# One store of eight rows instead of two of four, in a decode kernel fed by one stream of loads

## The chip, the cores and the metric

The kernel runs on one core of one Trainium2 chip. Its time is the device time of one execution in microseconds; smaller is better. Five engines work side by side: TensorE (PE, with its weight loads listed apart as PEld), VectorE (DVE), ScalarE (ACT), GpSimd (POOL) and SyncE (SP). SP and ACT each have a queue on which they issue transfers, and all transfers run on the same 16 DMA engines. SBUF and PSUM are the core's memories of 128 partitions (rows).

## What is computed

One decode step of a transformer block for two sequences, in float32. `x` has shape (2, 1, 512). It is normalised, and three terms are added:

```python
xn = _layernorm(x, axis=-1)
return x + _A_ref(xn, K, V, wq, wo) + _B_ref(xn, w_gate, w_up, w_down)
```

The term A is attention with 32 heads of 128: `q = xn @ wq`, scores of q against the last 2048 of 8192 cached keys, softmax, the weighted sum of the cached values, and `@ wo`. The term B is `((xn @ w_gate) * (xn @ w_up)) @ w_down` with 1376 inner columns. For each of the 2 x 32 pairs of sequence and head some 1 MB of keys and 1 MB of values is read once. With the weights that is 159.5 MB to load, and 4 KB to store.

## The kernel before

**The stream.** The host lays caches and weights out in the order of use, in one array `stream`. `blocks()` (line 38) lists the pieces: keys of head h, values of head h - 3 (`LAG`), the slices of `wq` and `wo` that go with them, and at the end the pieces of `w_down` (`wd`). `pump()` (line 139) issues these loads on SP's queue into a ring of three step tiles, each of 55,296 bytes on each partition. `done()` (line 164) counts the users of a tile and calls `pump()` when a tile is free. The first load, `wq0`, has a tile of its own. The last load, `wd_rest`, brings the last 96 rows of `w_down`.

**The order on an engine.** `InOrder` (line 73) keeps each engine's instructions in the order in which they are written; all calls through it appear in the profile as line 85. POOL is not wrapped, so its lines (181, 198, 278, 294) appear by themselves. The main loop (line 400) takes one head's keys, multiplies them on DVE by q (`products`, in place), sums over the 128 columns (`sums`), takes maxima, and lets ACT make the exponentials into a ring of tiles `p`. The head's values follow three heads later on PE (`weigh`, `pv`). `transpose(h)` then picks the two sequences' rows with a small table of ones, `pick`, and ACT scales them into `oT`, of 128 rows and 2 columns, the weights of `project_o`.

**The sum.** `project_o` sums into two rows (one for each sequence) of the PSUM tile `acc`, 512 columns wide, for the heads before `HF` = 26. Then the sum is spread: `accumulate` (line 300) cuts the 512 columns into four groups g of 128 and writes group g to the rows 32 g and 32 g + 1, so that four narrow matmuls use four parts of the array. The sum so far is copied to `acc_sb` and put in through the identity. The last heads and all of `w_down` (`down`, with `hT` as weights) go this way. `keep_busy` issues matmuls whose result is not used.

**The two ends.** `x_t` (line 122) is one tile with three parts, brought by one load on ACT's queue: x with its 512 columns spread over partitions (`xT`, 8 columns), x in the rows 32 g + b where the result will stand (`x_nat`, 128 columns, zero elsewhere), and `pick` (8 columns). The mean and variance come from `xT`, then `xn` and its copies `xnb`, which PE uses for the first q. At the end DVE adds `x_nat` to the whole spread sum, 128 by 128 (line 474), and the result leaves in two stores, one for each sequence, of four rows of 512 bytes each: sequence 0 on SP's queue, sequence 1 on ACT's.

Of the kernel before, what the change touches and what calls it, by code (L numbers as in the profile page):

```python
# [8 lines left out]
F32 = mybir.dt.float32  # L9
AF = mybir.ActivationFunctionType  # L10
# [6 lines left out]
P = 128  # L17
B, D, H, DH, SK, F = 2, 512, 32, 128, 8192, 1376
W = min(4096, max(256, SK // 4))
J = W // P  # L20
NC = D // P
FB = 4 * P
NFB = -(-F // FB)
NFC = F // P
FR = F - NFC * P
FH = [(0, 2 * FB), (2 * FB, F)]
LAG = 3
HG = 4
GC = HG * DH
JG = J // 4  # L30
# [7 lines left out]
def blocks():  # L38
# [6 lines left out]
    def k(h):  # L45
        first = [("w", 1, CQ - NC * DH)] if h == 0 else []
        return [("k", h, CK)] + first + ([("wq", h, CP)] if h + HG < H else [])

    def v(h):
        return [("v", h, CK), ("wo", h, CO)]  # L50

    def gu(half):
        n = NC * (FH[half][1] - FH[half][0])
        return [("wg", half, n), ("wu", half, n)]

    units = []
    for h in range(LAG, H - 1):
        units += [k(h), v(h - LAG)]
    loads = [k(0), gu(0) + k(1), gu(1) + k(2), units[0] + units[1]]
    loads += [sum(units[i : i + 3], []) for i in range(2, len(units), 3)]  # L60
    loads += [k(H - 1) + v(H - 1 - LAG)]
    out = [(("q", 0), [("w", 0, NC * DH)])]
# [38 lines left out]
def kernel(  # L101
    ctx: ExitStack,
    tc: tile.TileContext,
    x: bass.AP,
    stream: bass.AP,
    wd_rest: bass.AP,
    out: bass.AP,
):
    nc = tc.nc
    pe, dve, act, sp = (InOrder(tc, e) for e in (nc.tensor, nc.vector, nc.scalar, nc.sync))  # L110
# [3 lines left out]
    const = ctx.enter_context(tc.tile_pool(name="const", bufs=1))  # L114
    steps = ctx.enter_context(tc.tile_pool(name="steps", bufs=BUFS))
    small = ctx.enter_context(tc.tile_pool(name="small", bufs=6))
# [2 lines left out]

    x_t = const.tile([P, B * NC + P + 4 * B], F32, name="x_t")
    act.dma_start(x_t, x)
    xT = x_t[:, 0 : B * NC].rearrange("p (b c) -> p b c", b=B)
    x_nat = x_t[:, B * NC : B * NC + P]
    pick = x_t[:, B * NC + P :].rearrange("p (r b) -> p r b", b=B)


    todo, at = [], 0
# [34 lines left out]
    def done(kind, i):  # L164
# [14 lines left out]
    ident = const.tile([P, P], F32, name="ident")  # L179
    nc.gpsimd.memset(ident, 1.0)  # L180
    nc.gpsimd.affine_select(
        out=ident, in_=ident, compare_op=ALU.is_equal, fill=0.0, base=0,
# [2 lines left out]

    acc_t = ps_c.tile([P, D], F32, name="acc")
    dve.memset(acc_t, 0.0)
    acc, acc_g = acc_t[:B, :], acc_t[:, :P]

    o_ps = [ps_c.tile([P, 4 * DH], F32, name=f"o_ps{i}") for i in range(2)]  # L190
    for t in o_ps:
# [2 lines left out]

    NP = LAG + 2
    p_ring = [const.tile([P, B, JG, 4 * B], F32, name=f"p{i}") for i in range(NP)]
    for t in p_ring:
        nc.gpsimd.memset(t, 0.0)


# [24 lines left out]
    q_ps, s_t, mm_t, p_t, sum_t, rec_t, o_sbs, oT = {}, {}, {}, {}, {}, {}, {}, {}  # L225
# [4 lines left out]
    def project_first(i):  # L230
        w = got["w", i][0].rearrange("p (c n) -> p c n", c=NC)
        if i == 0:
            q = q_first
        else:
            q_ps[0] = ps_q.tile([P, B, GC], F32, name="q")
            q = q_ps[0][:, :, DH:]
        for b in range(B):
            for c in range(NC):
                pe.matmul(
                    q[:, b, :], xnb[:, c * B + b, :], w[:, c, :],  # L240
                    start=(c == 0), stop=(c == NC - 1),
                )
        done("w", i)

    def project_q(h):

        g, c = h // HG + 1, h % HG
        if c == 0:
            q_ps[g] = ps_q.tile([P, B, GC], F32, name="q")
        for b in range(B):  # L250
            pe.matmul(
                q_ps[g][:, b, :], xnb[:, c * B + b, :], got["wq", h][0],
                start=(c == 0), stop=(c == NC - 1),
            )
        done("wq", h)

    def k_of(h):
        return got["k", h][0].rearrange("p (b j d) -> p b j d", b=B, j=J)

    def products(h):  # L260
        g, hh = divmod(h, HG)
        kt = k_of(h)
        qb = q_ps[g][:, :, hh * DH : (hh + 1) * DH] if h else q_first
        dve.tensor_tensor(
            kt, kt, qb.unsqueeze(2).to_broadcast([P, B, J, DH]), op=ALU.mult
        )
# [33 lines left out]
    def accumulate(lhsT, rhs, last=False):  # L300
        nonlocal n_acc
        for g in range(4):
            pe.matmul(
                acc_g[32 * g : 32 * g + B, :], lhsT, rhs[:, g * P : (g + 1) * P],
                start=(n_acc == 0), stop=last,
            )
        n_acc += 1

    def keep_busy(n):
        pe.matmul(spare[:, 0:n], mean_w, spare_in[:, 0:n], start=True, stop=True)  # L310
# [14 lines left out]
    def transpose(h):  # L325
        o_sb, rec = o_sbs.pop(h), rec_t.pop(h)
        d = tr[:, 8 + 4 * (h % 2) : 8 + 4 * (h % 2) + B]
        for r in range(4):
            pe.matmul(
                d, o_sb[:, r * DH : (r + 1) * DH], pick[:, r, :],  # L330
                start=(r == 0), stop=(r == 3),
            )
        oT[h] = small.tile([P, B], F32, name="oT")
        for b in range(B):
            act.activation(
                oT[h][:, b : b + 1], d[:, b : b + 1], AF.Copy, scale=rec[:, b : b + 1]
            )

    def project_o(h):
        wo = got["wo", h][0]  # L340
        if h < HF:
            pe.matmul(acc, oT.pop(h), wo, start=(h == 0), stop=(h == HF - 1))
        else:
            accumulate(oT.pop(h), wo)
        done("wo", h)
# [15 lines left out]
        project_o(h)  # L361


    hT = const.tile([P, 4, 4, B], F32, name="hT")

    def project_gu(half):
        lo, hi = FH[half]
# [12 lines left out]
    def gate():  # L380
        g_sb = small.tile([P, FB], F32, name="o_sb", bufs=2)
        act.copy(g_sb, gu_ps[0])
        h_sb = small.tile([P, FB], F32, name="o_sb", bufs=2)
        dve.tensor_tensor(h_sb, g_sb, gu_ps[1], op=ALU.mult)
        for i in range(4):
            t = tr[:, (i % 3 + 1) * P : (i % 3 + 2) * P]
            pe.transpose(t, h_sb[:, i * P : (i + 1) * P], ident)
            act.copy(
                hT[:, i, :, :], t.rearrange("p (n r) -> p n r", r=32)[:, :, 0:B]
            )  # L390

    def down(n):
# [7 lines left out]
    for _, fields in blocks()[1:]:  # L400
# [6 lines left out]
        for n, h in enumerate(ks):  # L407
            products(h)
            if h == 0:
                project_first(1)  # L410
            if h + HG < H:
                project_q(h)
# [14 lines left out]

    h = H - 2
    spare = ps_q.tile([P, B, GC], F32, name="q")[:, 0, :]
    acc_sb = const.tile([B, D], F32, name="acc_sb")  # L430
    dve.tensor_copy(acc_sb, acc)
    products(h)
    sums(h)
# [1 line left out]
    pv(HF + 1)  # L435
    keep_busy(GC)
    transpose(HF)
    accumulate(ident[:B, :B], acc_sb)
    keep_busy(256)
    project_o(HF)  # L440
    transpose(HF + 1)
# [30 lines left out]
    accumulate(hT[:FR, NFC % 4, NFC // 4, :], got["wd", NFC][0][:FR], last=True)  # L472
    o_out = const.tile([P, P], F32, name="o_out")
    dve.tensor_tensor(o_out, acc_g, x_nat, op=ALU.add)
    for b, eng in ((0, sp), (1, act)):
        eng.dma_start(out[b, 0, :].rearrange("(g n) -> g n", n=P), o_out[b::32, :])


def laid_out(x):

    import numpy as np

    a = x["A_x"].reshape(B, D)
    xs = np.zeros((P, B * NC + P + 4 * B), a.dtype)
    xs[:, : B * NC] = a.reshape(B, P, NC).transpose(1, 0, 2).reshape(P, B * NC)
    for b in range(B):
        xs[b::32, B * NC : B * NC + P] = a[b].reshape(D // P, P)
        for r in range(4):
            xs[4 * b + r :: 32, B * NC + P + r * B + b] = 1.0
    cache = {  # L490
        kind: x[name][:, :, SK - W :, :].reshape(B, H, P, J * DH).transpose(1, 2, 0, 3)
        for kind, name in (("k", "A_k_cache"), ("v", "A_v_cache"))
    }
    wq = x["A_wq"].reshape(P, NC, H // HG, GC).transpose(2, 0, 1, 3)
    wo = x["A_wo"].reshape(H, P, D)
    gu = {
        kind: x[name].reshape(P, NC, F)
        for kind, name in (("wg", "B_w_gate"), ("wu", "B_w_up"))
    }
    wd = x["B_w_down"]  # L500

    def field(kind, i):
        if kind in ("k", "v"):
            return cache[kind][i].reshape(P, CK)
        if kind in ("v0", "v1"):
            return cache["v"][i].reshape(P, B, -1)[:, int(kind[1])]
        if kind == "w":
            return (wq[0][:, :, DH:] if i else wq[0][:, :, :DH]).reshape(P, -1)
        if kind == "wq":
            return wq[i // HG + 1][:, i % HG, :]  # L510
        if kind == "wo":
            return wo[i]
        if kind == "wd":
            return wd[i * P : (i + 1) * P]
        return gu[kind][:, :, FH[i][0] : FH[i][1]].reshape(P, -1)

    parts = [
        np.concatenate([field(kind, i) for kind, i, _ in fields], axis=1).ravel()
        for _, fields in blocks()
    ]  # L520
    return {"x": xs, "stream": np.concatenate(parts), "wd_rest": wd[NFC * P :]}


_INS = ["A_x", "A_k_cache", "A_v_cache", "A_wq", "A_wo", "B_w_gate", "B_w_up", "B_w_down"]
# [28 lines left out]
```

## Time and profile before

| | |
|---|---|
| median of 3 runs | 380.98 us (380.95 to 381.12) |
| profiled execution | 380.88 us, span 378.8 us |
| PE busy | 264.5 us (70%) |
| DVE busy | 293.9 us (78%) |
| ACT busy | 64.0 us (17%) |
| POOL busy | 25.4 us (7%) |
| read from HBM | 159.52 MB, 421 GB/s over the span |

The page gives the busy time of each engine, then the span in 40 slices with one digit each (the busy share in tenths), then the DMA queues with their packets, bytes and share of 16 DMA engines' time: q1 is SP's queue, q10 ACT's. A group of instructions is written as line, engine, operation, output <- inputs, with shapes as partitions x elements; after the bar stand the busy time and the mean of one in nanoseconds, and then the idle time of the engine just ahead of them with what ended it. In an extract in order of time the columns are start and duration in microseconds, engine, line, operation, tiles, and in square brackets the idle time before it. The span is the profiled part of an execution; 2.1 us of the time lie around it.

### The profile page before, as it was taken

To read this page: it belongs to the slowest core of one execution; us is meant where nothing else is said; L and a number is where in the kernel's file an instruction comes from. 1 tells how busy PE (TensorE), PEld (TensorE's weight loads), DVE (VectorE), ACT (ScalarE), POOL (GpSimd) and SP (SyncE) were. 2 spreads that over 40 slices of the span, in tenths; PEclk is the share of its full clock that TensorE was granted. 3 is DMA by queue.
4 is the path that set the end of the run, shared out by engine and by line. 5 is a ranking of instruction groups with operands and counts; after the bars stand their busy time and mean duration, and the time that the engine had idled before them with its cause. 6 is when DMAs were issued, how large, how long until landed. Compare 5 with 4: busy or idle time off the path is not lost.

```text
span 378.8 us, 3075 instructions
## 1 busy us (share of the span) xinstructions
PE 264.5 (70%) x1188; PEld 92.7 (24%) x1188; DVE 293.9 (78%) x143; ACT 64.0 (17%) x264; POOL 25.4 (7%) x75
## 2 busy tenths in 40 slices
PE   3949882757838875684886668488477847719996
PEld 3512221212212221221222122122112311203342
DVE  3739892996799499589949949994994998699920
ACT  1020020102101110210121121021203112202221
POOL 0000000000000000000000000010000000000000
PEclk9978985868876696986679687768958879757999
DMA  8999999999999999999999999999999999999993
GB/s 321 458 419 435 438 445 444 403 444 461 389 450 450 403 455 420 428 455 403 439 457 391 455 450 393 461 421 426 455 415 428 455 423 433 400 445 408 426 415 146
DMA packets 4893, 159.71 MB, mean 422 GB/s; under 512 B 552, under 2 KB 688, under 8 KB 1296
## 3 DMA queue, kind: packets, MB, share of 16 engines
q1 hardware_dynamic: 4728, 159.45, 98.0%
q8 instruction: 9, 0.15, 0.2%
q10 hardware_dynamic: 152, 0.08, 0.1%
q14 instruction: 4, 0.03, 0.0%
HBM read 159.52 MB, written 0.00 MB: 421 GB/s over the span
## 4 chain that ended last, share of the span: by engine, by line
DMA 54%; DVE 31%; PE 11%; ACT 2%; issue 1%; SPq 0%; POOL 0%; DVEq 0%
DMA step<-in_stream_dram 54%; DVE s L85 15%; DVE step L85 15%; PE acc L85 3%; PE o_ps L85 3%; PE q L85 2%; PE tr L85 2%; ACT o_sb L85 1%; ACT oT L85 1%; DVE m L85 0%; SPq L85 0%; ACT p L85 0%; DVE rec L85 0%; POOL mm L278 0%; DVE acc_sb L85 0%
## 5 line engine op out<-in xcount | busy, mean ns | idle before, releaser
L85 DVE TENSOR_TENSOR step<-step,q 128x4096 f32<-128x4096 f32 x31 | 136.6, 4407 | 57.8 <-DMA step<-in_stream_dram 52.4
L85 DVE TENSOR_REDUCE s<-step 128x32 f32<-128x4096 f32 x32 | 141.4, 4420 | 1.1
L85 PE MATMUL q<-step,xnb 128*128 128x512 f32 (+1 forms) x128 | 91.9, 864 | 58.2 <-DMA step<-in_stream_dram 58.1
L85 PE MATMUL o_ps<-step,p 128*8 128x512 f32 x512 | 85.1, 725 | 8.2 <-DMA step<-in_stream_dram 8.0
L85 PEld LDWEIGHTS q<-step,xnb 128*128 128x128 f32 x128 | 32.1, 274 | 112.8 <-issue 55.7
L85 PE MATMUL tr<-x_t,o_sb 128*128 128x2 f32 x256 | 33.3, 252 | 22.9 <-ACT o_sb L85 22.8
L85 PE MATMUL acc<-step,oT 128*2 128x512 f32 (+1 forms) x100 | 38.2, 535 | 13.1 <-ACT oT L85 13.1
L85 PEld LDWEIGHTS tr<-x_t,o_sb 128*128 128x128 f32 x256 | 31.2, 191 | 51.3 <-ACT o_sb L85 50.6
L85 ACT COPY o_sb<-o_ps 128x512 f32<-128x512 f32 x33 | 19.2, 583 | 114.0 <-PE o_ps L85 114.0
L85 PEld LDWEIGHTS o_ps<-step,p 128*8 128x8 f32 x512 | 14.0, 97 | 73.6 <-issue 62.4
L85 ACT ACTIVATE nm<-mm 128x2 f32<-128x2 f32 x32 | 6.5, 203 | 147.2 <-POOL mm L278 147.2
L278 POOL PARTITION_ALL_REDUCE mm<-m x32 | 11.4, 357 | 285.4 <-DVE rec L85 184.4
L85 ACT ACTIVATE oT<-tr,rec 128x1 f32<-128x1 f32 x64 | 13.2, 257 | 37.6 <-PE tr L85 37.6
L85 ACT ACTIVATE p<-s,nm 128x16 f32<-128x16 f32 x64 | 19.2, 300 | 1.0
L294 POOL PARTITION_ALL_REDUCE sum<-rs x32 | 12.8, 400 | 41.6 <-ACT p L85 41.6
L85 ACT ACTIVATION_READ_ACCUMULATOR p<-s,nm 128x1 f32 x64 | 12.0, 187 | 0.0
L85 PE MATMUL o_ps<-step,xn 128*2 128x512 f32 (+1 forms) x48 | 11.9, 548 | 0.0
L85 PE MATMUL q<-xnb,mean_w 128*128 128x512 f32 (+1 forms) x24 | 11.9, 584 | 0.0
L85 DVE TENSOR_TENSOR o_out<-acc,x_t 128x128 f32<-128x128 f32 x1 | 0.3, 292 | 11.3 <-PE acc L85 11.3
L85 DVE TENSOR_TENSOR step<-step,tr 128x4096 f32<-128x4096 f32 x1 | 4.4, 4420 | 4.4 <-DMA step<-in_stream_dram 4.4
L85 PEld LDWEIGHTS acc<-step,oT 128*2 128x2 f32 x100 | 3.1, 82 | 17.9 <-ACT oT L85 16.8
L85 DVE TENSOR_REDUCE m<-s 128x2 f32<-128x32 f32 x32 | 5.9, 186 | 1.1
(36 smaller groups left out, 37.9 us busy)
## 6 DMA issues: line engine op xcount, KB each, us to landing
step<-in_stream_dram SPq DMA_DIRECT2D x16, 6912.0 KB, 31.7
step<-in_stream_dram SPq DMA_DIRECT2D x2, 6400.0 KB, 30.6
step<-in_stream_dram SPq DMA_DIRECT2D x1, 6656.0 KB, 29.2
step<-in_stream_dram SPq DMA_DIRECT2D x1, 4608.0 KB, 25.3
step<-in_stream_dram SPq DMA_DIRECT2D x2, 2304.0 KB, 13.5
step<-in_stream_dram SPq DMA_DIRECT2D x1, 4352.0 KB, 24.9
step<-in_stream_dram SPq DMA_DIRECT2D x1, 3712.0 KB, 33.8
step<-in_stream_dram SPq DMA_DIRECT2D x1, 3072.0 KB
```

What stands on the lines that cost most here:

```text
L85: made = call(*args, **kwargs)
L278: nc.gpsimd.partition_all_reduce(mm, m, P, bass_isa.ReduceOp.max)
L294: nc.gpsimd.partition_all_reduce(sum_t[h], rs, P, bass_isa.ReduceOp.add)
```

## The change

The result leaves in one store of eight rows on SP. For that, sequence 1 is summed in row 32 g + 16 of `acc` rather than 32 g + 1, so that the rows wanted are every 16th. The weights of these sums get 17 columns rather than 2, where columns 1 to 15 are zero: `oT` becomes a ring of three tiles cleared once by POOL, `hT` grows from 2 to 17 columns for each chunk and is cleared once by DVE, `acc_sb` has 17 rows and the identity is 17 by 17. The one load of `x_t` is cut into four on ACT's queue: `x_t` (128 rows of 32 bytes), `pick` (the same size), and four rows of 512 bytes for each sequence into `x_nat`, which DVE clears first.

```diff
+RB = 16
+M = RB * (B - 1) + 1
...
-    x_t = const.tile([P, B * NC + P + 4 * B], F32, name="x_t")
+    x_t = const.tile([P, B * NC], F32, name="x_t")
     act.dma_start(x_t, x)
...
+    pick_t = const.tile([P, 4 * B], F32, name="pick")
+    act.dma_start(pick_t, picks)
+    pick = pick_t.rearrange("p (r b) -> p r b", b=B)
+    x_nat = const.tile([P, P], F32, name="x_nat")
+    dve.memset(x_nat, 0.0)
+    for b in range(B):
+        act.dma_start(x_nat[RB * b :: 32, :], x_rows[b])
...
-    acc, acc_g = acc_t[:B, :], acc_t[:, :P]
+    acc, acc_g = acc_t[:M, :], acc_t[:, :P]
...
+    oT_ring = [const.tile([P, M], F32, name=f"oT{i}") for i in range(3)]
+    for t in oT_ring:
         nc.gpsimd.memset(t, 0.0)
...
-                acc_g[32 * g : 32 * g + B, :], lhsT, rhs[:, g * P : (g + 1) * P],
+                acc_g[32 * g : 32 * g + M, :], lhsT, rhs[:, g * P : (g + 1) * P],
...
-        oT[h] = small.tile([P, B], F32, name="oT")
+        oT[h] = oT_ring[h % 3]
         for b in range(B):
             act.activation(
-                oT[h][:, b : b + 1], d[:, b : b + 1], AF.Copy, scale=rec[:, b : b + 1]
+                oT[h][:, RB * b : RB * b + 1], d[:, b : b + 1], AF.Copy, scale=rec[:, b : b + 1]
             )
...
-    hT = const.tile([P, 4, 4, B], F32, name="hT")
+    hT = const.tile([P, 4, 4, M], F32, name="hT")
+    dve.memset(hT, 0.0)
...
-                hT[:, i, :, :], t.rearrange("p (n r) -> p n r", r=32)[:, :, 0:B]
+                hT[:, i, :, ::RB], t.rearrange("p (n r) -> p n r", r=32)[:, :, 0:B]
...
-    acc_sb = const.tile([B, D], F32, name="acc_sb")
+    acc_sb = const.tile([M, D], F32, name="acc_sb")
...
-    accumulate(ident[:B, :B], acc_sb)
+    accumulate(ident[:M, :M], acc_sb)
...
-    for b, eng in ((0, sp), (1, act)):
-        eng.dma_start(out[b, 0, :].rearrange("(g n) -> g n", n=P), o_out[b::32, :])
+    sp.dma_start(out.rearrange("b o (g n) -> (o g) b n", n=P), o_out[::RB, :])
```

The host hands over `x`, `picks` and `x_rows` as three arrays in place of one.

More of the change, by code (lines that the diff above doesn't have):

```diff
@@ L104 @@
     x: bass.AP,
+    picks: bass.AP,
+    x_rows: bass.AP,
     stream: bass.AP,
@@ L118 @@
     ps_c = ctx.enter_context(tc.tile_pool(name="ps_c", bufs=1, space=bass.MemoryType.PSUM))
-    x_t = const.tile([P, B * NC + P + 4 * B], F32, name="x_t")
+    x_t = const.tile([P, B * NC], F32, name="x_t")
     act.dma_start(x_t, x)
-    xT = x_t[:, 0 : B * NC].rearrange("p (b c) -> p b c", b=B)
-    x_nat = x_t[:, B * NC : B * NC + P]
-    pick = x_t[:, B * NC + P :].rearrange("p (r b) -> p r b", b=B)
+    xT = x_t.rearrange("p (b c) -> p b c", b=B)
+    pick_t = const.tile([P, 4 * B], F32, name="pick")
[5 more added lines that the diff above has]
+        act.dma_start(x_nat[RB * b :: 32, :], x_rows[b])
     todo, at = [], 0
@@ L197 @@
     for t in p_ring:
+        nc.gpsimd.memset(t, 0.0)
+    oT_ring = [const.tile([P, M], F32, name=f"oT{i}") for i in range(3)]
+    for t in oT_ring:
         nc.gpsimd.memset(t, 0.0)
@@ L483, in laid_out @@
     a = x["A_x"].reshape(B, D)
-    xs = np.zeros((P, B * NC + P + 4 * B), a.dtype)
-    xs[:, : B * NC] = a.reshape(B, P, NC).transpose(1, 0, 2).reshape(P, B * NC)
+    xs = a.reshape(B, P, NC).transpose(1, 0, 2).reshape(P, B * NC)
+    picks = np.zeros((P, 4 * B), a.dtype)
     for b in range(B):
-        xs[b::32, B * NC : B * NC + P] = a[b].reshape(D // P, P)
         for r in range(4):
-            xs[4 * b + r :: 32, B * NC + P + r * B + b] = 1.0
+            picks[4 * b + r :: 32, r * B + b] = 1.0
     cache = {
@@ L520, in laid_out @@
     ]
-    return {"x": xs, "stream": np.concatenate(parts), "wd_rest": wd[NFC * P :]}
+    return {
+        "x": xs, "picks": picks, "x_rows": a.reshape(B, D // P, P),
+        "stream": np.concatenate(parts), "wd_rest": wd[NFC * P :],
+    }
 _INS = ["A_x", "A_k_cache", "A_v_cache", "A_wq", "A_wo", "B_w_gate", "B_w_up", "B_w_down"]
```

## The prediction

> **What bounds the kernel now.** I read the page's slices and queues first, then the chain that ended last, and then the two ends of the run, where the change sits. The slices and the queues:
>
> ```profile
> span 378.8 us, 3075 instructions
> DMA  8999999999999999999999999999999999999993
> q1 hardware_dynamic: 4728, 159.45, 98.0%
> q10 hardware_dynamic: 152, 0.08, 0.1%
> DMA 54%; DVE 31%; PE 11%; ACT 2%; issue 1%; SPq 0%; POOL 0%; DVEq 0%
> ```
>
> The load queue (q1) fills 98.0% of 16 DMA engines' span and only the first and last slices are not full. The chain names 31% of DVE because it follows the release of a buffer back to DVE, but the DMA row shows that the transfers never wait for that release: loads of 6912 KB land 31.7 us after they are issued although 6912 KB at 422 GB/s last 16.8 us, so about one load always stands in the queue ahead. The time is therefore a start (until the stream runs), the stream, and a tail (from the last landing to the end). Work that neither delays the stream nor lies in the tail is worth nothing.
>
> The tail, from the order of time and from stretches of 0.1 us (columns of these: PE, PEld, DVE, ACT, POOL, clock, DMA share, GB/s), and what SP waits for at the end:
>
> ```profile
> 375.03 0.11 PEld L85 LDWEIGHTS acc<-step,hT 96*2 96x2 f32 x8 [0.29 <-DMA step<-in_wd_rest_dram]
> 375.50 0.29 DVE L85 TENSOR_TENSOR o_out<-acc,x_t 128x128 f32<-128x128 f32 x1 [11.29 <-PE acc L85]
> 375.82 0.65 SPq L85 DMA_DIRECT2D out_dram<-o_out  x1
> 375.82 1.36 ACTq L85 DMA_DIRECT2D out_dram<-o_out  x1
> ```
>
> ```profile
> 377.00:377.10 0.10, 0.00 (x0) 0.00 (x0) 0.00 (x0) 0.00 (x0) 0.00 (x0) 1.00 0.07 15
> 377.10:377.20 0.10, 0.00 (x0) 0.00 (x0) 0.00 (x0) 0.00 (x0) 0.00 (x0) 1.00 0.04 5
> 377.20:377.30 0.10, 0.00 (x0) 0.00 (x0) 0.00 (x0) 0.00 (x0) 0.00 (x0) 1.00 0.00 0
> 377.30:377.40 0.10, 0.00 (x0) 0.00 (x0) 0.00 (x0) 0.00 (x0) 0.00 (x0) 1.00 0.10 21
> ```
>
> ```profile
> SPq L549 <- DMA out_dram<-o_out: 1.3, 1, 1.3
> ```
>
> The last load, `wd_rest`, releases PE at 375.03. Eight matmuls and the addition follow, and both stores are issued at 375.82. SP's issue ends at 376.47, ACT's only at 377.18. Two bursts of 2 KB show: 377.0 to 377.2 and 377.3 to 377.4. I take the first for SP's rows, as its issue ended first. SP then waits 1.3 us, until about 377.8: the landing of the second burst. From there to 378.8 is 1.0 us of closing, which the change does not name.
>
> The start:
>
> ```profile
> 0.79 0.39 SPq L85 DMA_DIRECT2D wq<-in_stream_dram  x1
> 0.80 0.41 ACTq L85 DMA_DIRECT2D x_t<-in_x_dram  x1
> 1.24 1.28 ACT L85 ACT_TABLE_LOAD   x1 [1.24 <-PEq L535]
> 1.25 20.68 SPq L85 DMA_DIRECT2D step<-in_stream_dram  x4
> 4.03 0.16 DVE L85 TENSOR_REDUCE st<-x_t 128x2 f32<-128x8 f32 x1 [1.30 <-DMA x_t<-in_x_dram]
> 11.94 4.42 DVE L85 TENSOR_TENSOR step<-step,tr 128x4096 f32<-128x4096 f32 x1 [4.44 <-DMA step<-in_stream_dram]
> ```
>
> x is needed first at 4.03, but the first big product waits for the stream until 11.94, so what depends on x has cover.
>
> **The change part by part**, against the profiled execution (380.88 us, a span of 378.8 and 2.1 around it; the median of the runs shown is 380.98, 0.10 above).
>
> 1. *Store.* ACT's store goes, and SP's carries eight rows of 512 B. If the eight rows move where SP's four moved, the last landing comes 0.27 us earlier (first bursts at about 377.05 and 377.32). Best end: ACT's issue had slowed SP's; alone it takes 0.34, as the issue of `wd_rest` at 356.57 did, rather than 0.65, and another 0.31 goes: -0.6. Worst end: eight rows take as long to issue as ACT's 1.36, and rows start as long after the issue's end as SP's did (376.47 to 377.05, 0.58): 375.82 + 1.36 + 0.58 = 377.76, 0.44 after the old second burst: +0.45. I take -0.27: SP's own store on the same queue is the nearest row, and four rows more are 2 KB, one burst of 0.1 us at most.
>
> 2. *x in four loads.* 72 KB become 4 + 4 + 2 + 2 = 12 KB; 60 KB less at 430 GB/s is -0.14 us of stream. Against this stand small packets: q10's 4.0% of 16 engines in the first 6 us is 3.84 us for 144 packets, 27 ns each. The 128 rows become 256 rows of 32 B and 8 of 512 B; with the loads' closing packets (16 above the 128 rows before) some 304 in all, 160 more, 4.3 us over 16 engines: at most +0.27. Between -0.14 and +0.27 I take 0, since a 32 B packet should cost less than a 576 B one but not nothing.
> On ACT's queue three more issues stand ahead of the table load: 0.41 for the pick table and 0.65 to 1.36 each for the two of four rows, so the table load ends at 4.2 to 5.7 rather than 2.5. The square root behind it ran at 6.11 after 3.59 us of idle. Cover: at least 0.4 us; if that were gone, q of head 0 (PE from 7.57 to 11.35) still has 0.5 us before the load that ends DVE's wait at 11.94, and behind that the queue's spare load. Cost 0. ACT's two row loads wait for the memset of `x_nat`, first on DVE (0.17, the row of `mean_w`) and over at 1.05, before ACT's second issue ends. Only the last addition reads `x_nat`.
>
> 3. *Memsets.* On DVE `x_nat` delays the other memsets by 0.17, where DVE then waits 1.30 for x; `hT` (272 columns, between the 165 ns of 128 and the 485 ns of 512) falls into the 4.44 us before 11.94. On POOL three of 17 columns, at most 146 ns each (the row of 128x64): the first maximum over partitions moves from 23.24 to at most 23.7. Behind it wait ACT's exponentials and DVE's first reciprocal, which comes after the sums of head 1 at 36.2. All hidden; without cover +0.8 in all.
>
> 4. *17 columns of weights.* A weight load takes 82 ns with 2 columns, 97 with 8 and 191 with 128; 17 should be some 95. The pitch does not follow it: 24 matmuls of 128 columns by 2 took 0.84 us (35 ns), eight of 512 by 8 took 1.04 us (32.5 ns per 128). From the last landing eight matmuls count: 0 to 8 x 13 = 0.1. If every load from 372.93 on showed, 64 x 13 = 0.8, less the 0.9 us of waits for landings (0.29, 0.33, 0.29) inside. I take +0.02. The wide `acc` matmuls of the middle lie beside the stream, as do `hT`'s strided copies (166 ns each); the copy of `acc` (659 ns) is as long with 17 partitions as with 2.
>
> 5. *Ring of three oT.* Its writer waits for the projection three heads before, long done: 0.
>
> Sum: -0.27 + 0 + 0.02 = -0.25, so 380.63, called 380.6.
>
> One rule speaks against part 2. The Trainium skill, "DMA: Bandwidth & Descriptors", section "Bandwidth", says that transfers under 64 KB are mostly descriptor overhead and should be merged; its section on one DMA's anatomy gives about 2 us of fixed cost each. By it the sum would gain 6 us if the three extra loads stood in a row on the path; here the 72 KB load landed in 3.2 us and its first user has the cover named, so the trace makes it nothing. A rule speaks on part 1 too: the same page, section "Issuing engines are not separate DMA queues", says that issuing on two engines saves sequencer time alone. By it the second store bought nothing but its issue; the trace agrees so far that its burst came 0.27 us late.
>
> **The rivals.**
> - *The issue gets shorter too.* For it: no other issue of SP's in the rows quoted is above 0.5 us, and ACT's took 1.36 beside it. Against: at 0.79 the two issued side by side in 0.39 and 0.41. Part 1's best end with part 2's best: 380.88 - 0.6 - 0.14 - some 0.1 of closing waits passed early = 380.05.
> - *Nothing is won.* Eight rows are issued as slowly as ACT's four; 0 to +0.45: 380.9 to 381.35. For it: the store's 0.65 is not explained by rows (128 rows took 0.39), so a wider pattern may cost more.
> - *Slower: the stream starts late.* The place is the first big step load, issued at 1.25 when ACT now issues the pick table. If the two queues' issues are served one after another, and the small loads get ahead, the load begins 0.41 + 2 x 0.65 = 1.7 us later: 380.88 + 1.7 - 0.25 = 382.3. It decides once the delay passes 1.0 us. For it: two stores issued together took 0.65 and 1.36, as if one waited for the other. Against: at 0.79 they did not, and SP's issue at 1.25 stands before the ACT issue that can only follow 1.21.
>
> **How the numbers follow.** No change is told from a change by this kernel's times within about 0.2%, 0.76 us. Forecast 0.43 (its own range 380.3 to 380.9), shorter issue 0.30, nothing won 0.12, late stream 0.15. Faster than 380.22 takes the shorter issue and little of the forecast: 0.32. Within 0.2%: 0.53. Slower than 381.74: 0.15. The range takes in the shorter issue down to 379.8 and "nothing won", and leaves most of the late stream out: 379.8 to 381.6.
>
> **What would show it.** Right: one issue of the store near 0.65 us, one burst near 1.2 us after it, SP's wait ending some 0.3 us earlier relative to `o_out`, and the load stream beginning and ending at the same times. The shorter issue shows as 0.35 to 0.45 us. The late stream shows as DMA slices below full between 2 and 5 us and a later first product than 11.94. Wrong: `wd_rest` released at another time than about 375.0, or a pitch of the last matmuls well above 35 ns.

## The result and the profile after

The changed kernel takes 380.35 us (median of 14 runs, 380.04 to 382.01), the kernel before in the same call 381.08 us (380.69 to 381.25). The ratio is 0.9983, with a 95% interval of 0.9976 to 0.9990: 0.65 us less, between 0.38 and 0.91. The interval does not hold 1, so there is a gain; its size is below the 0.2% (0.76 us) under which the prediction would not speak of a change. The forecast was 380.6, a gain of 0.25, and that is less than the interval's smaller end.

The page of the changed kernel, in the lines that answer to those of before (the span, the DMA row, the two load queues, the shares of the chain):

```profile
span 378.4 us, 3087 instructions
DMA  8999999999999999999999999999999999999994
q1 hardware_dynamic: 4732, 159.46, 98.2%
q10 hardware_dynamic: 304, 0.01, 0.0%
DMA 60%; DVE 24%; PE 12%; ACT 2%; SPq 1%; issue 1%; POOL 0%; DVEq 0%
```

Nothing has changed in kind: the load queue still fills all slices but the two at the ends (98.2% where it was 98.0%). q10, ACT's queue, has the 304 packets that were counted beforehand.

The tail of the changed kernel in order of time, then its stretches of 0.1 us (the last two columns are the DMA share and GB/s), then SP's wait for the store:

```profile
374.86 0.13 PEld L87 LDWEIGHTS acc<-step,hT 96*17 96x17 f32 x8 [0.25 <-DMA step<-in_wd_rest_dram]
375.35 0.29 DVE L87 TENSOR_TENSOR o_out<-acc,x_nat 128x128 f32<-128x128 f32 x1 [11.21 <-PE acc L87]
375.67 0.69 SPq L87 DMA_DIRECT2D out_dram<-o_out  x1
```

```profile
376.90:377.00 0.10, 0.00 (x0) 0.00 (x0) 0.00 (x0) 0.00 (x0) 0.00 (x0) 1.00 0.10 26
377.00:377.10 0.10, 0.00 (x0) 0.00 (x0) 0.00 (x0) 0.00 (x0) 0.00 (x0) 1.00 0.08 16
377.10:377.20 0.10, 0.00 (x0) 0.00 (x0) 0.00 (x0) 0.00 (x0) 0.00 (x0) 1.00 0.00 0
```

```profile
SPq L567 <- DMA out_dram<-o_out: 0.9, 1, 0.9
```

One issue of 0.69 us stands where two stood (0.65 and 1.36), one burst of 4.2 KB where there were two of 2 KB, and it starts 1.29 us after the issue starts, where the first one stood at 1.24. SP's wait is 0.9 us, not 1.3. (Distances of this kind are taken here and below from the trace's own records, which have three digits after the point.) From the issue's start to the end of the span it is 2.70 us, where it was 3.00. That is 0.30 us, near the forecast's 0.27, but it is made up otherwise. The last packet of the store lands 1.41 us after the issue's start, where it was 1.61, so the landing gives 0.20; the other 0.10 is in what follows the landing (1.29 us, where it was 1.38), which the forecast took as fixed. The issue itself also stands earlier, at 375.67 rather than 375.82, because `wd_rest` lands earlier (374.86, not 375.03). That part was not in the sum. One execution doesn't show it, though: seven profiled executions with the step tiles where the kernel before has them and the stream issued at the same time (that of before, and six of the kernels below) have that landing anywhere from 374.86 to 375.21.

The start of the changed kernel, in order of time:

```profile
0.79 0.41 ACTq L87 DMA_DIRECT2D x_t<-in_x_dram  x1
1.24 0.45 ACTq L87 DMA_DIRECT2D pick<-in_picks_dram  x1
1.25 1.36 SPq L87 DMA_DIRECT2D step<-in_stream_dram  x3
1.73 1.63 ACTq L87 DMA_DIRECT2D x_nat<-in_x_rows_dram  x2
3.39 1.28 ACT L87 ACT_TABLE_LOAD   x1 [3.39 <-DVE o_ps L87]
12.03 4.42 DVE L87 TENSOR_TENSOR step<-step,tr 128x4096 f32<-128x4096 f32 x1 [4.52 <-DMA step<-in_stream_dram]
```

ACT is busy issuing until 3.36, its table load follows at 3.39, and the first big product starts at 12.03, 0.09 us later than before. So the gain is not at the start. The median span is 0.6 us shorter (378.3 us, where the kernel before has 378.9) and the tail 0.30, so it is not all in the tail either; some of it is in the stream between.

### The profile page after: what moved, and what is told of

It reads as the page before. It is cut to its first block, busy times and chain, and to the rows that moved or that the text cites. A ratio compares the mean times of both kernels' runs of the same rounds, so it can differ in the third digit from the quotient of the medians.

```text
span 378.4 us, 3087 instructions
## 1 busy us (share of the span) xinstructions
PE 260.7 (69%) x1188; PEld 93.1 (25%) x1188; DVE 294.4 (78%) x145; ACT 63.9 (17%) x264; POOL 25.4 (7%) x78
## 3 DMA queue, kind: packets, MB, share of 16 engines
q1 hardware_dynamic: 4732, 159.46, 98.2%
## 4 chain that ended last, share of the span: by engine, by line
DMA 60%; DVE 24%; PE 12%; ACT 2%; SPq 1%; issue 1%; POOL 0%; DVEq 0%
DMA step<-in_stream_dram 60%; DVE s L87 12%; DVE step L87 12%; PE o_ps L87 5%; PE q L87 3%; PE acc L87 2%; PE tr L87 1%; SPq L87 1%; ACT o_sb L87 1%; ACT oT L87 1%; DVE m L87 0%; ACT p L87 0%; DVE acc_sb L87 0%; DVE rec L87 0%; POOL mm L292 0%
## 5 line engine op out<-in xcount | busy, mean ns | idle before, releaser
L87 PE MATMUL q<-step,xnb 128*128 128x512 f32 (+1 forms) x128 | 89.6, 846 | 60.4 <-DMA step<-in_stream_dram 60.4
L87 PE MATMUL o_ps<-step,p 128*8 128x512 f32 x512 | 82.1, 697 | 8.0 <-DMA step<-in_stream_dram 7.8
L87 PEld LDWEIGHTS q<-step,xnb 128*128 128x128 f32 x128 | 31.3, 267 | 115.4 <-DMA step<-in_stream_dram 57.0
L87 PE MATMUL tr<-pick,o_sb 128*128 128x2 f32 x256 | 33.7, 254 | 24.8 <-ACT o_sb L87 24.7
L87 PE MATMUL acc<-step,oT 128*17 128x512 f32 (+1 forms) x100 | 38.3, 538 | 13.4 <-ACT oT L87 13.4
L87 PEld LDWEIGHTS tr<-pick,o_sb 128*128 128x128 f32 x256 | 31.7, 193 | 53.2 <-ACT o_sb L87 52.5
L87 PE MATMUL o_ps<-step,xn 128*2 128x512 f32 (+1 forms) x48 | 13.0, 597 | 0.0
L87 PEld LDWEIGHTS acc<-step,oT 128*17 128x17 f32 x100 | 4.1, 98 | 18.1 <-ACT oT L87 15.1
```

Of the source, the lines that this page charges most:

```text
L87: made = call(*args, **kwargs)
```

## The experiments

Three questions were open. Was the gain in the tail what it was thought to be, one landing in place of two? What else moved the end of the stream? And does the cut of x into four loads cost anything? The theory of the forecast says that the store is everything. Its rival came from the addresses. The change makes `hT` (128 to 1088 bytes on each partition) and the ring of `oT` (0 to 288) larger, and both lie ahead of the ring of step tiles in SBUF, so the ring moves by 1248 bytes: its start is 224 bytes past a multiple of 256 before and 192 past one after, by adding up the tiles ahead of it, each rounded up to 32 bytes. (Each step tile has 216 x 256 bytes, so its three tiles stand alike.) By this rival the position of the ring sets how long its loads take.

All runs in one table. "Ring" is the start of the step tiles in bytes past a multiple of 256. The ratio is to the kernel before in the same call (medians there 380.98 to 381.08), with its 95% interval. The span is the median over the kernel's runs, and "outside" the median of time less span. The last column is the profiled execution's span less the start of the store's issue, from the trace's records.

| kernel | ring | ratio | median us | span | outside | issue to end |
|---|---|---|---|---|---|---|
| before | 224 | 1 | 380.98 to 381.08 | 378.9 | 2.08 | 3.00 |
| changed | 192 | 0.9983 (0.9976 to 0.9990) | 380.35 | 378.3 | 1.98 | 2.70 |
| after_224 | 224 | 0.9990 (0.9982 to 0.9999) | 380.68 | 378.5 | 2.13 | 2.69 |
| after_pad | 0 | 0.9951 (0.9939 to 0.9964) | 379.19 | 377.1 | 2.06 | 2.71 |
| before_pad | 0 | 0.9961 (0.9948 to 0.9973) | 379.54 | 377.5 | 2.06 | 3.00 |
| before_128 | 128 | 0.9993 (0.9984 to 1.0001) | 380.72 | 378.7 | 2.05 | 3.00 |
| store_224 | 224 | 0.9984 (0.9975 to 0.9993) | 380.48 | 378.7 | 1.72 | 2.81 |
| store_pad | 0 | 0.9954 (0.9940 to 0.9967) | 379.12 | 377.3 | 1.71 | 2.80 |
| x_loads | 224 | 0.9998 (0.9989 to 1.0007) | 380.88 | 378.8 | 2.13 | 2.82 |
| wide | 224 | 0.9997 (0.9988 to 1.0005) | 380.97 | 378.8 | 2.10 | 3.01 |
| two_on_sp | 224 | 1.0003 (0.9994 to 1.0012) | 381.12 | 379.3 | 1.81 | 3.36 |
| two_on_sp_x2 | 224 | 1.0005 (0.9996 to 1.0014) | 381.15 | 379.1 | 2.01 | 3.31 |
| act_none | 224 | 0.9998 (0.9989 to 1.0007) | 381.11 | 379.3 | 1.78 | 2.80 |
| small_x_pad | 0 | 0.9955 (0.9942 to 0.9967) | 379.52 | 377.5 | 2.02 | 2.78 |

### The ring put back, and put on a multiple of 256 bytes

An unused tile behind `hT` moves the ring, with the tiles behind it, and does no work. In the changed kernel 8 columns, 32 bytes, put it back at 224 (after_224); 16 columns put it on a multiple of 256 (after_pad):

```diff
     hT = const.tile([P, 4, 4, M], F32, name="hT")
+    const.tile([P, 8], F32, name="pad")
```

> The changed kernel with 32 bytes per partition added ahead of the ring of step tiles, so that the ring starts as far past a multiple of 256 bytes as it did before the change (224 bytes; the changed kernel has 192). Theory A, the forecast's: the gain is the store (0.3 us) and at most 0.15 us of x, and the place of the ring does nothing: 380.35 us, ratio to the kernel before 0.9981. Theory B: the moved ring shortened every row of the stream by about 1 ns (2048.6 to 2047.3 ns for 55,296 bytes, some 295 rows on each DMA engine, so 0.3 us), and that is the part of the gain that the forecast lacks: 380.65 us, ratio 0.9989, and mean rows of 2048.6 ns again.

> The changed kernel with 64 bytes per partition added ahead of the ring, which then starts at a multiple of 256 bytes. Theory A: 380.35 us, as the changed kernel. Theory B: if each 32 bytes nearer to the multiple take 1 ns from a row, 6 steps from 192 to 0 take 6 ns from each of some 295 rows on an engine, 1.8 us: 378.6 us, ratio 0.9935. If only part of the 1.3 ns was due to the place, between the two.

The same in the kernel before, where 8 columns put the ring on a multiple of 256 (before_pad) and 40 columns 128 past one (before_128):

```diff
     hT = const.tile([P, 4, 4, B], F32, name="hT")
+    const.tile([P, 8], F32, name="pad")
```

> The kernel before with 32 bytes per partition added ahead of the ring, which then starts at a multiple of 256 bytes (224 past one before); nothing of the change is in it. Theory A: no difference, 381.08 us. Theory B: 7 steps of 32 bytes, 7 ns from each of some 295 rows: 2.1 us less, 379.0 us, ratio 0.9946.

> The kernel before with 160 bytes per partition added ahead of the ring, which then starts 128 bytes past a multiple of 256 (224 before, 0 in the run with 32 bytes added). If a row costs time in proportion to the bytes past the multiple: 128/224 of the 5.3 ns that the rows of 55,296 bytes lost stay, so rows of some 2046.3 ns, 0.65 us less, 380.35 us, ratio 0.9983. Rival, only a start at a multiple of 256 counts: 2048.5 ns and 381.0 us, no difference. Rival, 128 is as good as 256: 2043.3 ns, 379.5 us.

With the ring on a multiple of 256 the kernel before is 1.5 us faster and the changed one 1.2 us faster than without; after_pad's interval (0.9939 to 0.9964) lies wholly below that of the changed kernel, which begins at 0.9976. Both differences come from an unused tile. Each is smaller than expected (2.1 and 1.8 us, at 1 ns a transfer for every 32 bytes). The tail of before_pad, then that of after_pad, in order of time:

```profile
374.37 0.29 DVE L85 TENSOR_TENSOR o_out<-acc,x_t 128x128 f32<-128x128 f32 x1 [10.94 <-PE acc L85]
374.69 0.65 SPq L85 DMA_DIRECT2D out_dram<-o_out  x1
374.70 1.36 ACTq L85 DMA_DIRECT2D out_dram<-o_out  x1
```

```profile
373.55 0.13 PEld L87 LDWEIGHTS acc<-step,hT 96*17 96x17 f32 x8 [0.20 <-DMA step<-in_wd_rest_dram]
374.04 0.29 DVE L87 TENSOR_TENSOR o_out<-acc,x_nat 128x128 f32<-128x128 f32 x1 [10.75 <-PE acc L87]
374.36 0.69 SPq L87 DMA_DIRECT2D out_dram<-o_out  x1
```

The last addition starts 1.13 us earlier than in the kernel before (374.37, not 375.50) and 1.31 us earlier than in the changed one (374.04, not 375.35), and what follows it is as long as it was: the issue's 0.65 and 1.36, or 0.69, and 3.00 or 2.71 us to the end. The gain lies wholly ahead of the tail. In the middle of the run, from 50 to 300 us, where the DMA engines are full in each kernel, the last column (GB/s) shows it; before and then before_pad:

```profile
50.00:300.00 250.00, 172.99 (x678) 55.10 (x676) 202.13 (x90) 41.95 (x177) 16.64 (x44) 0.77 1.00 431
```

```profile
50.00:300.00 250.00, 171.05 (x688) 56.63 (x687) 203.22 (x90) 42.16 (x179) 16.61 (x45) 0.78 1.00 433
```

The DMA share is 1.00 in both, so there were no gaps to fill: the same bytes move in less time. The records of the 2,048 transfers of 55,296 bytes say how much, as mean and median of each profiled execution:

```
ring past 256 B   mean ns            median ns
224               2048.3 to 2048.7   2045   (all eight kernels at 224)
192               2047.3             2044   (changed)
128               2046.8             2042   (before_128)
0                 2043.1 to 2043.3   2041   (after_pad, store_pad, before_pad)
0                 2045.0             2041   (small_x_pad)
```

The means hold a few slow transfers: 9 to 40 of the 2,048 took over 2,060 ns, and 90 in small_x_pad, whose median is that of the others at 0. It is the place past a multiple of 256 that goes with the durations, not the address as such: kernels at 224 stand at two addresses 1280 bytes apart, and so do those at 0.

From 224 to 0 it is 5.3 ns by the means and 4 by the medians. A DMA engine handles 4,192 / 16 = 262 rows of the stream (nearly all the rest of q1's 4,728 packets are 4-byte packets that close a transfer), and if each gains as much, that is an estimate of 1.0 to 1.4 us; 1.5 was measured in the kernel before and 1.2 in the changed one. From 224 to 192, the change's own step, it is 1.0 to 1.3 ns, an estimate of 0.3 us; the medians of after_224 and the changed kernel are 0.33 us apart. Their intervals overlap, so of the step of 32 bytes it is shown only that the transfers are shorter; that it is worth 0.33 us is an estimate that fits. So too at 128: the transfers are shorter, but the time of before_128 is not told from that of before (0.9984 to 1.0001). With the ring put back at 224 the change gains 0.38 us (0.04 to 0.69), and that interval holds the 0.25 of the forecast.

The Trainium skill, "DMA: Bandwidth & Descriptors", section "How a descriptor splits into AXI transactions", says that a transfer which does not start on a multiple of 256 bytes fetches from the multiple below, so that the bytes between cost beats of 32 bytes that bring nothing: 7 beats at 224, 6 at 192, 4 at 128. The rule tells of what is fetched; the ring is where the bytes are written, so it is carried over here. With 55,296 bytes (1,728 beats) in some 2,043 ns a beat would be 1.18 ns, an estimate, and by the rule 224 to 0 would be 8.3 ns (5.3 measured by the means, 4 by the medians), 224 to 192 1.2 (1.0 to 1.3, and 1), 224 to 128 3.5 (1.8, and 3). The order agrees, the size for the smallest step, but not for the whole; the measurements decide.

### The store alone, and its parts

The store of eight rows, with all that it needs (row 32 g + 16, 17 columns, the memsets), and with x in one load as before; the ring at 224 by 8 unused columns (store_224), and on a multiple of 256 by 16 (store_pad):

```diff
-    x_t = const.tile([P, B * NC], F32, name="x_t")
+    x_t = const.tile([P, B * NC + P + 4 * B], F32, name="x_t")
     act.dma_start(x_t, x)
...
-    act.dma_start(pick_t, picks)
...
-    for b in range(B):
-        act.dma_start(x_nat[RB * b :: 32, :], x_rows[b])
...
+    const.tile([P, 8], F32, name="pad")
```

> The changed kernel with x in one load of 72 KB as before (x in rows 32 g and 32 g + 16), and with the ring 224 bytes past a multiple of 256 as before: the store, the wide weights and the memsets alone. Theory A: -0.3 us from the store, 380.8 us, ratio 0.9992. Rival, the gain is that of x in small loads: 381.1 us, ratio 1.000. Rival, the store is worth more than its landing (the whole measured gain of 0.73 us): 380.35 us.

> The store of eight rows with x in one load as before, and the ring of step tiles moved to a multiple of 256 bytes (it was 224 past one in the run with the store alone). If the three parts add: the span of the store alone (378.7 us) less the 1.5 to 1.9 us that the moved ring took in the two kernels where it was tried, 376.9 to 377.2 us, and the 1.73 us outside the span that the store alone showed (2.08 before): 378.6 to 378.9 us, ratio 0.9940, faster than every kernel so far. Rival: the short time outside the span belongs to that one program and not to the store; then 2.06 outside, 379.0 to 379.3 us.

The end of store_224, in order of time and among SP's waits:

```profile
375.11 0.13 PEld L87 LDWEIGHTS acc<-step,hT 96*17 96x17 f32 x8 [0.24 <-DMA step<-in_wd_rest_dram]
375.91 0.70 SPq L87 DMA_DIRECT2D out_dram<-o_out  x1
```

```profile
SPq L562 <- DMA out_dram<-o_out: 1.0, 1, 1.0
```

From the issue to the end of the span it is 2.81 us, 0.19 less than before, and that is the landing's 0.20 again (1.41 us after the issue's start, not 1.61); what follows the landing is as long as before (1.39 us). The median span is 0.2 to 0.3 us shorter. That agrees with the store's term. The time outside the span is 0.36 us shorter besides, which no theory had named (see "The time outside the span"). store_pad and after_pad are alike to 0.07 us, so, within their intervals, nothing is lost where the four loads go and x comes as before.

The 17 columns without the store (`wide`: the kernel before with rows 32 g + 16, 17 columns, the memsets, and both stores kept; the ring at 224 by the same 8 columns):

```diff
     for b, eng in ((0, sp), (1, act)):
-        eng.dma_start(out[b, 0, :].rearrange("(g n) -> g n", n=P), o_out[b::32, :])
+        eng.dma_start(out[b, 0, :].rearrange("(g n) -> g n", n=P), o_out[RB * b :: 32, :])
```

> The rows 32 g and 32 g + 16 with weights of 17 columns, the memsets and the ring of oT, but x in one load and two stores on SP and ACT as before, the ring of step tiles 224 bytes past a multiple of 256 as before. Forecast: +0.02 to +0.1 us, 381.06 to 381.2 us; the last eight matmuls take 0.44 to 0.55 us. Rival, the narrow weight loads carry part of the gain, or the cleared tiles shorten the time outside the span: 380.7 us.

The end of `wide` in order of time, and its group of weight loads (busy us, mean ns of one, idle before them):

```profile
375.01 0.13 PEld L87 LDWEIGHTS acc<-step,hT 96*17 96x17 f32 x8 [0.26 <-DMA step<-in_wd_rest_dram]
375.50 0.29 DVE L87 TENSOR_TENSOR o_out<-acc,x_t 128x128 f32<-128x128 f32 x1 [11.31 <-PE acc L87]
375.82 1.36 ACTq L87 DMA_DIRECT2D out_dram<-o_out  x1
```

```profile
L87 PEld LDWEIGHTS acc<-step,hT 128*17 128x17 f32 x80 | 1.8, 97 | 0.6 <-DMA step<-in_stream_dram 0.4
```

A weight load of 17 columns takes 97 ns, and from the landing of `wd_rest` to the last addition it is 0.49 us, 0.02 more than before. The time is that of before: ratio 0.9997.

The two stores, both on SP:

```diff
-    for b, eng in ((0, sp), (1, act)):
+    for b, eng in ((0, sp), (1, sp)):
```

> The kernel before with both stores of four rows on SP, one after the other; nothing else. If the landing alone counts: SP's second issue ends 0.65 us after the first (377.1 us), its rows move 0.6 us later and land 0.4 us after, 378.1 us against 377.76, so the span rises by 0.2 to 0.4 to 379.3 us. If a store on ACT's queue costs time outside the span, that falls from 2.08 to 1.73: 381.0 us in all; if not, 381.4 us.

Its end in order of time, and four of its stretches of 0.1 us:

```profile
375.92 1.21 SPq L85 DMA_DIRECT2D out_dram<-o_out  x2
```

```profile
377.10:377.20 0.10, 0.00 (x0) 0.00 (x0) 0.00 (x0) 0.00 (x0) 0.00 (x0) 1.00 0.06 15
377.20:377.30 0.10, 0.00 (x0) 0.00 (x0) 0.00 (x0) 0.00 (x0) 0.00 (x0) 1.00 0.04 5
377.70:377.80 0.10, 0.00 (x0) 0.00 (x0) 0.00 (x0) 0.00 (x0) 0.00 (x0) 1.00 0.07 15
377.80:377.90 0.10, 0.00 (x0) 0.00 (x0) 0.00 (x0) 0.00 (x0) 0.00 (x0) 1.00 0.04 5
```

SP's two issues take 0.65 and 0.51 us one after the other, the bursts stand 0.6 us apart rather than 0.3, and from the issue to the end it is 3.36 us, 0.36 more than with two queues and 0.66 more than with the changed kernel's one store. An SP store of four rows takes 0.65 us with no ACT beside it, so ACT's issue had not slowed it. The second queue had saved 0.36 us at the end, less than the 0.51 of an issue. The rule of the Trainium skill quoted with the forecast ("DMA: Bandwidth & Descriptors", section "Issuing engines are not separate DMA queues") says that a second issuing engine saves only the time to issue. The trace agrees so far: on one queue the second issue starts when the first is over, and its burst comes 0.6 us behind the first, not 0.3.

### x in four loads

The loads alone, in the kernel before (rows b, both stores; the host hands over three arrays):

```diff
-    x_t = const.tile([P, B * NC + P + 4 * B], F32, name="x_t")
+    x_t = const.tile([P, B * NC], F32, name="x_t")
     act.dma_start(x_t, x)
...
+    pick_t = const.tile([P, 4 * B], F32, name="pick")
+    act.dma_start(pick_t, picks)
...
+    x_nat = const.tile([P, P], F32, name="x_nat")
+    dve.memset(x_nat, 0.0)
+    for b in range(B):
+        act.dma_start(x_nat[b :: 32, :], x_rows[b])
```

> The kernel before with x in four loads alone: two stores, two columns, ring where it was. If the four loads are worth what the two runs with and without them differ by (span 378.57 against 378.74, outside 2.12 against 1.73): the span falls by 0.2 to 378.8 us, the time outside rises by up to 0.4 from 2.08, 380.9 to 381.3 us. Rival of the forecast, late stream: a later first product than 11.94 us and a span of 379.5 or more. Rival, the time outside does not know of the loads: 380.9 us.

Its two stores in order of time, and its two bursts:

```profile
376.00 0.65 SPq L85 DMA_DIRECT2D out_dram<-o_out  x1
376.00 0.58 ACTq L85 DMA_DIRECT2D out_dram<-o_out  x1
```

```profile
377.20:377.30 0.10, 0.00 (x0) 0.00 (x0) 0.00 (x0) 0.00 (x0) 0.00 (x0) 1.00 0.10 21
377.50:377.60 0.10, 0.00 (x0) 0.00 (x0) 0.00 (x0) 0.00 (x0) 0.00 (x0) 1.00 0.08 16
```

By themselves the loads cost nothing that shows: ratio 0.9998. This run also settles a reading of the forecast. ACT's issue took 0.58 us, not 1.36, and ended before SP's. The packets show that now ACT's burst (queue q10) came first and SP's (q1) 0.3 us after it, although the two issues ended only 0.06 us apart. So the second burst of before was not late because ACT's issue was long.

What a later start of the stream would cost, in store_224 with the load of x moved from ACT's queue to the head of SP's:

```diff
-    act.dma_start(x_t, x)
+    sp.dma_start(x_t, x)
```

> The store of eight rows alone (ring 224 bytes past a multiple of 256), with the one load of x moved from ACT's queue to the head of SP's, so that ACT issues nothing. If each of the first two transfers on ACT's queue costs 0.35 us outside the span: 1.4 us outside; if only the second does: 1.73 as with one. The span: wq and the first step load are issued 0.45 us later, 378.7 to 379.2 us, as the stream starts by so much later or not. 380.1 to 380.9 us.

The start of store_224, then that of act_none, in order of time:

```profile
11.56 4.42 DVE L87 TENSOR_TENSOR step<-step,tr 128x4096 f32<-128x4096 f32 x1 [4.00 <-DMA step<-in_stream_dram]
```

```profile
0.79 0.40 SPq L87 DMA_DIRECT2D x_t<-in_x_dram  x1
1.26 0.41 SPq L87 DMA_DIRECT2D wq<-in_stream_dram  x1
12.52 4.42 DVE L87 TENSOR_TENSOR step<-step,tr 128x4096 f32<-128x4096 f32 x1 [5.86 <-DMA step<-in_stream_dram]
```

With one issue more ahead of the stream the first step load is issued 0.45 us later (at 1.71), and the median span is 0.6 us longer (the ratios, 0.9975 to 0.9993 and 0.9989 to 1.0007, overlap a little). The first product stands 0.96 us later, but that says little: in the other kernels it starts anywhere from 11.49 to 12.50, with the first step load issued at the same time. A late stream does cost about what it is late; the four loads on ACT's queue did not make it late.

### The time outside the span

store_224, store_pad and two_on_sp have 1.7 to 1.8 us of time outside the span, the others of the first eight tried 2.06 to 2.13, the changed kernel 1.98. The three have one transfer on ACT's queue in the whole program; the others have two or more. The theory was that a second transfer on ACT's queue costs 0.3 us at the program's end. Two kernels try it. two_on_sp with x brought by two loads on ACT:

```diff
-    act.dma_start(x_t, x)
+    act.dma_start(x_t[:, : B * NC], x[:, : B * NC])
+    act.dma_start(x_t[:, B * NC :], x[:, B * NC :])
...
-    for b, eng in ((0, sp), (1, act)):
+    for b, eng in ((0, sp), (1, sp)):
```

> The kernel before with both stores on SP, and x brought by two loads on ACT's queue (its 8 columns, then the other 136) rather than one. With one load on ACT and no store there the time outside the span was 1.80 us; in every kernel with two or more transfers on ACT's queue it was 2.02 to 2.13. Theory: the second transfer on ACT's queue makes the difference, whatever it is: 2.1 us outside, a span of 379.3, 381.4 us. Rival, it is the place or kind of the transfer (a store at the end, or small rows): 1.8 outside, 381.1 us.

And the changed kernel with the ring on a multiple of 256, one load of x and `pick` on ACT's queue, and `x_nat` by one load of eight rows on SP's queue behind the first loads of the stream:

```diff
-    x_t = const.tile([P, B * NC], F32, name="x_t")
+    x_t = const.tile([P, B * NC + 4 * B], F32, name="x_t")
     act.dma_start(x_t, x)
-    pick_t = const.tile([P, 4 * B], F32, name="pick")
-    act.dma_start(pick_t, picks)
...
-    for b in range(B):
-        act.dma_start(x_nat[RB * b :: 32, :], x_rows[b])
...
     pump()
+    sp.dma_start(x_nat[::RB, :], x_rows)
...
+    const.tile([P, 16], F32, name="pad")
```

> All that paid, together: the store of eight rows, the ring at a multiple of 256 bytes, x and the pick table in one small load (64 bytes a row) as the only transfer on ACT's queue, and the eight rows of x_nat in one load on SP behind the first four loads of the stream. The span of the changed kernel with the moved ring (377.1 us) plus the time outside with one transfer on ACT (1.75): 378.85 us, ratio 0.9943. Rival, the time outside does not follow ACT's queue: 379.2 us. Rival, the extra load on SP delays the fifth step load: it is issued after a wait of 20 us anyway, so no change.

The first agreed with the theory (2.01 us outside, where two_on_sp has 1.81). The second did not: it has one transfer on ACT's queue and still 2.02 us outside. act_none, with none, has 1.78. The theory falls, and the cause stays open. small_x_pad and store_pad also missed their forecasts (378.85, and 378.6 to 378.9; 379.52 and 379.12 came). small_x_pad is no faster than after_pad or store_pad; the three are alike within their intervals, and all beat both the changed kernel and the one before.

## Why the prediction was right, and where it was not

- *The sum's size.* Forecast 0.25 us of gain, measured 0.65 (0.38 to 0.91) by the ratio. The time is inside the range, above 380.22, and just inside the forecast's own 380.3 to 380.9. By the gain, the likeliest rival's price (0.83) is nearer than the forecast's, but not by its mechanism; by the time, 380.35 stands midway between the two (380.05 and 380.63). The term that the sum lacked is the place of the step tiles, worth some 0.3 us by the estimate above: it went through what the wider `hT` and the ring of `oT` do on the engines, and not through what they do to the addresses behind them. With the ring put back the gain is 0.38 (0.04 to 0.69).
- *Store, -0.27.* Right in kind: one burst at nearly the distance of the first, and SP's wait 0.9 us in place of 1.3. The landing came 0.20 us earlier, with the store alone too. That the whole tail of the changed kernel is 0.30 shorter, so near the forecast, is partly luck: another 0.10 is in what follows the landing, which was taken as fixed. It shows in the four kernels that load rows of x on ACT's queue and in no other; why is open.
- *"The issue gets shorter too".* Wrong as a mechanism: the eight rows took 0.69 us to issue, and SP's four rows alone 0.65. Its ground, that ACT's issue slowed SP's, fell with two_on_sp. (Its sum is 380.04, not 380.05, and the worst end of the store is 0.44, not 0.45.)
- *x in four loads, 0.* Right as far as the runs tell: 0.9998 alone. On top of the store (store_224 against after_224) the median span is 0.2 us shorter and the time outside it 0.4 longer, and the ratios' intervals overlap. The forecast also names some 2 us of fixed cost for each load. The Trainium skill, "DMA: Bandwidth & Descriptors", gives them in the section "Anatomy of one DMA — SWDGE (gpsimd) path" for transfers issued from GpSimd; the loads here are issued by ACT, and no such cost shows in the time. The table load ended at 4.67, within the 4.2 to 5.7 of the forecast, and the first product started at 12.03 (12.11 in x_loads), no later than in kernels with one load of x (11.56 to 12.14), so the covers named held.
- *17 columns, +0.02, and the memsets, 0.* Right: 97 ns for a weight load where some 95 were estimated, 0.49 us from the last landing to the addition in place of 0.47, ratio 0.9997 for `wide`.
- *"Nothing is won".* Its ground was that eight rows might take 1.36 us to issue; they took 0.69.
- *"The stream starts late".* It did not: the first step load was issued at 1.25 as before. act_none shows that its price was not far off, 0.6 us of span for 0.45 us of delay.
- *The 2.1 us around the span* were carried over unchanged. For the changed kernel that is nearly so (1.98), by luck: the store alone has 1.72. The cause is open.

From the medians, the way from before to the changed kernel is: span 378.9 to 378.7 with the store, to 378.5 with the four loads, to 378.3 with the ring moved, and 0.1 outside the span (where the steps are larger: 2.08, 1.72, 2.13, 1.98). Each single step is near the runs' spread; what is shown by separate intervals is the whole, and the effect of a ring on a multiple of 256 bytes. How much of the whole is the store and how much the ring is an estimate from the traces: 0.30 us in the tail and some 0.3 in the stream.

## What to carry to other kernels

Where a kernel is bound by a stream of loads, look at the duration of the single transfers and at the address to which they go: here one unused tile of 32 to 64 bytes, which put the ring on a multiple of 256 bytes, was worth 1.2 to 1.5 us (0.3 to 0.4%), more than the whole change. A change that makes a tile wider also moves every tile behind it, so compare changed and unchanged kernels with the addresses held equal before the difference is put down to the edit. And one store in place of two saves about the distance between their landings, here 0.2 us, not their issue.

## What was not expected of the hardware

- A transfer of 55,296 bytes on one partition takes 2,048.3 to 2,048.7 ns in the mean (median 2,045) when it goes to an address 224 bytes past a multiple of 256, and 2,043.1 to 2,043.3 (median 2,041) on a multiple. In small_x_pad the mean is 2,045.0 with the same median; why it has more slow transfers is open.
- The issue of the first transfer of four or eight rows on a queue is long and the next one short. On ACT it took 1.36 us in the kernel before, but 0.58 in x_loads, where ACT had issued two loads of four rows at the start, of 1.09 and 0.51. On SP it took 0.65 and then 0.51 in two_on_sp, and for eight rows 0.74 and then 0.61 in small_x_pad. Transfers of 128 rows took 0.39 to 0.45. That it is the first of its kind that costs was not tried by itself.
- With ACT's issue 0.78 us shorter in x_loads the bursts came at the same distances (1.2 and 1.5 us) from the issue's start, but in the other order, and the span ended 2.82 us after it, not 3.00 to 3.01 as in the four kernels whose ACT store took 1.36. Each of these is one profiled execution.
- From the landing of the last packet to the end of the span it is 1.23 to 1.29 us in the four kernels that load rows of x on ACT's queue at the start (x_loads, the changed kernel, after_224, after_pad), and 1.37 to 1.43 in the ten others. Why is open.
- The time outside the span is not a constant: 1.71 to 1.81 us in four kernels and 1.98 to 2.13 in the others, with the same stream. The number of transfers on ACT's queue does not explain it.
